# Reordering the opening of a fused attention and FFN kernel: casts, transposes, masks, table load and warm-up matmuls

## The chip, the cores and the metric

The kernel runs on one core of a Trainium2 chip. The core has TensorE (matmul, PE in the profile; its weight loads are PEld), VectorE (DVE), ScalarE (ACT), GpSimd (POOL) and SyncE (SP), which here only issues DMAs. The engines work through their own instruction queues in order and wait for one another by semaphores. The metric is the device time of one execution in microseconds (us), taken as the median over runs. Lower is better.

## The reference

A causal linear attention with decay is computed in blocks of 64 positions, with a running state per batch and head, and its output goes through a SwiGLU feed-forward layer:

```python
# q, k, v: (4 batches, 8 heads, 768 positions, 64); lam: one decay per head
for b in range(nb):                      # blocks of 64 positions
    intra = einsum('bhic,bhjc->bhij', qb, kb) * Dmask     # lam ** (i - j), causal
    intra = einsum('bhij,bhjd->bhid', intra, vb)
    inter = einsum('bhid,bhde->bhie', qb * lam_pow, kv_state)
    out[:, :, sl] = intra + inter
    kv_state = lam_block * kv_state + einsum('bhsd,bhse->bhde', kb * rev_pow, vb)
x = out.transpose(0, 2, 1, 3).reshape(3072, 512)
g = x @ w_gate                           # 512 x 1536
y = (silu(g) * (x @ w_val)) @ w_out      # 1536 x 512
```

Inputs and output are float32. The kernel multiplies in bfloat16 and accumulates in float32.

## The kernel before

The attention is done in 12 groups. A group is 256 positions of one batch with all 8 heads, held as two blocks of 128. The FFN is done in six steps of two groups each (512 tokens), with d_ff cut into 12 pieces of 128 columns (`fc`). For each piece TensorE makes the gate product (`ffn_gate`, L519) and the value product (`ffn_val`, L534) with four matmuls each; ScalarE applies silu (L523) and VectorE multiplies (L537). `ffn_out` (L552) multiplies by w_out.

The schedule is written out by hand: instructions go to each engine's queue in the order of the Python code, and the tile framework only adds semaphores. PSUM has eight banks, taken in a ring, and `ring[0] = n` sets where the ring goes on.

The opening is the part up to the list `steps`. It does groups 0 and 1 and the first two FFN pieces, while the loads are still coming in:

- **Loads.** SP issues lam, then k, q and v of groups 0 and 1 in halves of four heads, then weight pieces (`w_piece`). The two q halves of group 0 are issued from ScalarE's queue. Each half is 256 KB.
- **Warm-up.** TensorE starts with matmuls on constants: 30 tiny ones (L166, 8 columns), then `warm_up` ones of 512 columns (L131), with the small product that spreads lam over the partitions between them (L168). Later `warm_into` puts further constant matmuls of 256 columns (L172) between the real work.
- **Decay tables.** ScalarE takes the logarithm of lam (L180, L182) and then makes four tables `qdec` (L188), the factors `dec` for v (L614) and `lamgrp` for the state (L615) with exponentials. These need one activation table set; silu needs another, which is loaded by `preload_act_table_set("silu_and_others")` (L639).
- **Casts.** `cast_half(g, c, fns)` (L278) casts half `c` of k with `fns[0]` and of q with `fns[1]` to bfloat16; `None` leaves one out. `ACTC`, `DVEC` and `POOLC` are the copies of ScalarE, VectorE and GpSimd.
- **Transposes.** `pe_transpose(g, c, order, warm)` transposes on TensorE (L294). For k (`i == 0`) ScalarE copies the result out of PSUM (L296); for q (`i == 1`) VectorE does and multiplies by `qdec` (L300). `order` says which of the two comes first.
- **Scores and masks.** `scores` (L331) makes the products of q and k and leaves the causal masks (L338, VectorE) in a list; `run_later(n)` issues the next n of them.
- **v and state.** `v_scale` (L243, GpSimd) scales v by `dec`. `upd_mm` (L387) makes the state update of a group from k and the scaled v, and `upd_copy` copies it out on ScalarE: part 0 is `kvn` (L401), part 1 the two `ups` copies (L409). `state` (L426 to L437) goes on with them on GpSimd.
- **Output.** `intra` (L479) multiplies the masked scores by v, `inter` (L466) adds the part of the state. `guard` (L450) is a one-column copy on ScalarE that orders one after the other. `evac` (L491) copies the result into `xt`, the FFN's input.

## Time and profile before

| what | value |
|---|---|
| median of 5 runs | 228.05 us (227.53, 227.58, 228.05, 228.51, 229.45) |
| the profiled execution | 228.05 us |
| its span, first to last instruction | 226.3 us |
| TensorE busy in the span | 218.5 us |
| ScalarE, VectorE, GpSimd busy | 106.4, 90.8, 89.4 us |
| read from HBM, written | 28.31 MB, 6.29 MB |
| DMA share of 16 engines, in each microsecond from 3 to 15 | 1.04 to 1.15 |

The profile shows one execution. Times in it count from the start of the span. A row of the timeline gives start, duration, engine, source line, operation, the tile that is written and the one that is read, and in brackets how long the engine was idle before and what ended that. The durations of matmuls are modelled at their ends and overlap when matmuls are pipelined, so the distance of their starts says more than their sum.

### The profile page before, as it was taken

To read this page: it belongs to the slowest core of one execution; us is meant where nothing else is said; L and a number is where in the kernel's file an instruction comes from. 1 tells how busy PE (TensorE), PEld (TensorE's weight loads), DVE (VectorE), ACT (ScalarE), POOL (GpSimd) and SP (SyncE) were. 2 spreads that over 40 slices of the span, in tenths; PEclk is the share of its full clock that TensorE was granted. 3 is DMA by queue.
4 is the path that set the end of the run, shared out by engine and by line. 5 is a ranking of instruction groups with operands and counts; after the bars stand their busy time and mean duration, and the time that the engine had idled before them with its cause. 6 is when DMAs were issued, how large, how long until landed. Compare 5 with 4: busy or idle time off the path is not lost.

```text
span 226.3 us, 6040 instructions
## 1 busy us (share of the span) xinstructions
PE 218.5 (97%) x2504; PEld 122.6 (54%) x2504; DVE 90.8 (40%) x158; ACT 106.4 (47%) x211; POOL 89.4 (40%) x132
## 2 busy tenths in 40 slices
PE   8789999998999999999999999999999999999994
PEld 4566456886886555554544544544544444444442
DVE  2664358566753711733335262253242123222200
ACT  5878584854563353555454453453433423322321
POOL 6684737709593130979563092192150000000000
PEclk9999999999999999999999999999999999999999
DMA  6999999999997979396788838907101101101122
GB/s 196 345 330 363 369 353 322 241 156 303 402 262 161 245 209 269 77 226 167 180 194 217 217 83 219 247 3 139 49 1 46 49 0 46 46 3 46 46 93 93
DMA packets 88028, 39.70 MB, mean 175 GB/s; under 512 B 57666, under 2 KB 83522, under 8 KB 88002
## 3 DMA queue, kind: packets, MB, share of 16 engines
q1 hardware_dynamic: 83490, 32.58, 55.9%
q10 hardware_dynamic: 4512, 6.75, 8.2%
q8 instruction: 19, 0.31, 0.6%
q14 instruction: 7, 0.06, 0.1%
HBM read 28.31 MB, written 6.29 MB: 153 GB/s over the span
## 4 chain that ended last, share of the span: by engine, by line
PE 83%; DMA 8%; SPq 3%; POOL 3%; issue 1%; ACT 0%; DVE 0%; DVEq 0%; POOLq 0%
PE bank L552 28%; PE bank L519 25%; PE bank L534 24%; DMA v<-in_v_dram 8%; SPq L100 3%; POOL v_s L243 2%; PE bank L479 2%; PE bank L466 2%; PE bank L387 1%; PE bank L357 1%; PE bank L331 0%; PE bank L294 0%; POOL kvf L426 0%; POOL kvs L429 0%; ACT qkt L296 0%
## 5 line engine op out<-in xcount | busy, mean ns | idle before, releaser
L537 DVE TENSOR_TENSOR h<-sil,bank 128x512 bf16<-128x512 bf16 (+1 forms) x91 | 51.6, 575 | 103.9 <-PE bank L534 83.1
L519 PE MATMUL bank<-xt,wg_sb 128*128 128x512 bf16 (+1 forms) x364 | 77.2, 335 | 0.0
L534 PE MATMUL bank<-xt,wv_sb 128*128 128x512 bf16 (+1 forms) x364 | 77.1, 335 | 0.0
L523 ACT ACTIVATE sil<-bank 128x512 bf16<-128x512 f32 (+1 forms) x91 | 46.3, 514 | 42.6 <-PE bank L519 38.2
L552 PE MATMUL bank<-wo_sb,h 128*128 128x512 bf16 (+2 forms) x300 | 65.5, 371 | 0.0
L534 PEld LDWEIGHTS <-wv_sb 128*128 128x128 bf16 x364 | 35.5, 98 | 26.8
L519 PEld LDWEIGHTS <-wg_sb 128*128 128x128 bf16 x364 | 34.4, 98 | 26.0 <-DVE xt L491 0.2
L552 PEld LDWEIGHTS <-h 128*128 128x128 bf16 x300 | 28.7, 98 | 32.7
L554 ACT COPY osb<-bank 128x512 f32<-128x512 f32 (+1 forms) x24 | 14.0, 582 | 56.5 <-PE bank L552 56.5
L243 POOL TENSOR_TENSOR v_s<-v,dec 128x1024 bf16<-128x1024 f32 (+1 forms) x15 | 24.2, 1616 | 31.5 <-DMA v<-in_v_dram 31.3
L426 POOL TENSOR_TENSOR kvf<-kvs,ups 128x256 f32<-128x256 f32 x8 | 6.8, 849 | 29.5 <-ACT ups L409 26.8
L338 DVE TENSOR_TENSOR ssb<-bank,causal 128x512 bf16<-128x512 f32 x24 | 15.5, 684 | 4.6 <-PE bank L331 4.6
L491 ACT CAST xt<-bank 128x512 bf16<-128x512 f32 x19 | 11.6, 657 | 4.0 <-PE bank L479 3.1
L435 POOL CAST kvn<-kvf 64x256 bf16<-64x256 f32 x24 | 11.6, 482 | 1.5
L426 POOL TENSOR_TENSOR kvf<-kvf,ups 128x256 f32<-128x256 f32 x16 | 11.6, 724 | 0.6
L409 ACT COPY ups<-bank 128x256 f32<-128x256 f32 (+1 forms) x24 | 9.5, 450 | 1.4 <-PE bank L387 1.0
L263 ACT CAST qk<-kraw 128x1024 bf16<-128x1024 f32 x9 | 9.4, 1045 | 0.6 <-DMA qraw<-in_q_dram 0.5
L362 DVE TENSOR_TENSOR ssb<-bank,causaln 128x512 bf16<-128x512 f32 x12 | 8.2, 688 | 1.4 <-PE bank L357 1.3
L265 DVE TENSOR_TENSOR qk<-qraw,qdn 128x1024 bf16<-128x1024 f32 x6 | 7.6, 1267 | 2.0 <-DMA qraw<-in_q_dram 2.0
L387 PE MATMUL bank<-v_s,qk 64*64 64x64 bf16 x352 | 5.7, 195 | 1.8 <-POOL v_s L243 1.8
L479 PE MATMUL bank<-ssb,v_s 64*64 64x128 bf16 (+1 forms) x384 | 7.1, 207 | 0.3 <-ACT guard L450 0.3
L479 PEld LDWEIGHTS <-v_s 64*64 64x64 bf16 x384 | 5.7, 105 | 1.4 <-issue 0.7
(67 smaller groups left out, 121.5 us busy)
## 6 DMA issues: line engine op xcount, KB each, us to landing
out_dram<-osb ACTq DMA_DIRECT2D x23, 256.0 KB, 2.8
v<-in_v_dram SPq DMA_DIRECT2D x18, 256.0 KB, 4.5
woraw<-in_moe_w_out_dram SPq DMA_DIRECT2D x6, 512.0 KB, 8.1
kraw<-in_k_dram SPq DMA_DIRECT2D x24, 128.0 KB, 3.6
qraw<-in_q_dram SPq DMA_DIRECT2D x24, 128.0 KB, 3.4
wraw<-in_moe_w_gate_dram SPq DMA_DIRECT2D x5, 512.0 KB, 7.1
wraw<-in_moe_w_val_dram SPq DMA_DIRECT2D x5, 512.0 KB, 7.1
kraw<-in_k_dram SPq DMA_DIRECT2D x4, 512.0 KB, 6.4
```

What stands on the lines that cost most here:

```text
L243: eng.tensor_tensor(out=st[("vs", g)][:, h0:h1], in0=st[("v", g)][:, h0:h1].rearrange("p h (s d) -> p h s d", s=2), in1=vfac(g, h0, h1), o ...
L338: nc.vector.tensor_tensor(out=ssb[:, h2, 2 * c:2 * c + 2].rearrange("p a s n -> p a (s n)"), in0=sp[(c, h2)].rearrange("p (a x) -> p a x", ...
L426: nc.gpsimd.tensor_tensor(out=o, in0=f, in1=u, op=ALU.add)
L435: nc.gpsimd.tensor_copy(out=o[64 - h2 * 64:128 - h2 * 64], in_=f[h2 * 64:h2 * 64 + 64])
L479: nc.tensor.matmul(op[r][h2 * 64:h2 * 64 + 64, cols(g, hp, s)], v_s[ps, 2 * hp + h2, s], ssb[ps, h2, hp * 2 + s] if g >= NAT0 else ssb[ps, ...
L491: fns[r](out=xt[:, g % 2, :, r].rearrange("p h (m s) -> p h s m", s=2) if g < NAT0 else xt[:, g % 2, :, :, r * M:r * M + M], in_=op[r].rea ...
L519: nc.tensor.matmul(gp[:, 0:N], wg_sb[:, mc, fs], xt[:, b0 // 2:b1 // 2, mc].rearrange("p g b n -> p g (b n)"), start=(mc == 0), stop=(mc = ...
L523: nc.scalar.activation(sil[:, 0:N], gp[:, 0:N], AF.Silu)
L534: nc.tensor.matmul(vp[:, 0:N], wv_sb[:, mc, fs], xt[:, b0 // 2:b1 // 2, mc].rearrange("p g b n -> p g (b n)"), start=(mc == 0), stop=(mc = ...
L537: nc.vector.tensor_tensor(out=h_sb[:, fc % FH, b0:b1].rearrange("p b n -> p (b n)"), in0=sil[:, 0:N], in1=vp[:, 0:N], op=ALU.mult)
L552: nc.tensor.matmul(ps, st[("h", t, fc // FH)][:, fc % FH, b], wo_sb[:, fc, c0:c1], start=(fc == 0), stop=(fc == FC - 1))
L554: fn(out=osb[:, c0:c1], in_=ps)
```

## The change

All of it lies in the opening. No load, no shape and no arithmetic is changed.

- The lead-in has 40 tiny matmuls instead of 30, one 512-column warm-up ahead of the lam product instead of two, and three behind it instead of four.
- Group 0, first half: ScalarE casts k ahead of the first two `qdec` tables, not behind them. k is transposed ahead of q. The transposes stand ahead of the exponential of `dec`, and `lamgrp` moves behind the transposes of the second half.
- Group 0, second half: k is cast on GpSimd instead of ScalarE, and the two casts stand behind the first transposes.
- Of the constant matmuls of 256 columns between the real work, five go and three come in, two of those ahead of group 1's first transposes and one ahead of its last scores.
- The copy of group 0's state update (`upd_copy(0, (1,))`) moves up, to directly behind the first guard.
- Group 1, second half: the transposes of k and of q are taken apart; the load of the silu table set and `inter(0)` stand between them. The load stood ahead of `intra(0)`.
- The first gate weights are cast on VectorE instead of GpSimd.

```diff
--- before.py
+++ after.py
@@ -161,12 +161,12 @@
 
     lam_ps = bank()
     b = bank()
-    for n in range(30):
+    for n in range(40):
         r = slice(n % 2 * 64, n % 2 * 64 + 64)
         nc.tensor.matmul(b[r, 0:8], warm[r, 0:64], warm[r, 0:8], start=True, stop=True, skip_group_check=True)
-    warm_up(2)
+    warm_up(1)
     nc.tensor.matmul(lam_ps[:, 0:H], ones[:, 0:128], lam_row, start=True, stop=True)
-    warm_up(4)
+    warm_up(3)
     def warm_into(b, n, cols=256):
         for _ in range(n):
             nc.tensor.matmul(b[:, 0:cols], warm[:, 0:128], warm[:, 0:cols], start=True, stop=True)
@@ -607,55 +607,53 @@
     w_piece(1, 2)
     w_piece(2, 4)
     w_piece(4, 6)
-    cast_half(0, 0, (None, DVEC))
+    cast_half(0, 0, (ACTC, DVEC))
     qdec_table(0)
     qdec_table(1)
-    cast_half(0, 0, (ACTC, None))
+    ring[0] = 0
+    pe_transpose(0, 0, (0, 1), warm=1)
     nc.scalar.activation(dec, dec, AF.Exp)
-    nc.scalar.activation(lamgrp, lnp, AF.Exp, scale=float(2 * BLK))
-    cast_half(0, 1, (None, DVEC))
-    ring[0] = 0
-    pe_transpose(0, 0, warm=1)
-    cast_half(0, 1, (ACTC, None))
+    cast_half(0, 1, (POOLC, DVEC))
     qdec_table(2)
     qdec_table(3)
-    scores(0, (0,), 3)
+    scores(0, (0,), 2)
     run_later(1)
     v_scale(0, nc.gpsimd, 0, H // 2)
     v_scale(0, nc.gpsimd, H // 2, H)
     pe_transpose(0, 1)
+    nc.scalar.activation(lamgrp, lnp, AF.Exp, scale=float(2 * BLK))
     run_later(1)
     scores(0, (1,), 3)
     cast_half(1, 0, (ACTC, POOLC))
     run_later(1)
     ring[0] = 4
+    warm_into(banks[4], 2)
     pe_transpose(1, 0, (0,))
     ring[0] = 0
     up = [bank() for _ in range(2)]
-    warm_into(up[0], 1)
     upd_mm(0, up)
     run_later(1)
     upd_copy(0, (0,))
-    nc.scalar.preload_act_table_set("silu_and_others")
     ring[0] = 2
     st[("op", 0)] = [bank() for _ in range(2)]
     warm_into(st[("op", 0)][0], 1)
     ring[0] = 5
     pe_transpose(1, 0, (1,))
     cast_half(1, 1, (POOLC, POOLC))
-    warm_into(st[("op", 0)][0], 1)
     intra(0, True)
     guard(0)
+    upd_copy(0, (1,))
     ring[0] = 4
     scores(1, (0,))
     run_later(1)
     ring[0] = 6
-    pe_transpose(1, 1, (0, 1), warm=1)
+    pe_transpose(1, 1, (0,))
+    nc.scalar.preload_act_table_set("silu_and_others")
+    inter(0, False)
+    pe_transpose(1, 1, (1,))
     run_later(1)
-    inter(0, False)
-    upd_copy(0, (1,))
     ring[0] = 6
-    scores(1, (1,))
+    scores(1, (1,), 1)
     evac(0, (ACTC, ACTC))
     v_scale(1, nc.gpsimd, 0, H // 2)
     v_scale(1, nc.gpsimd, H // 2, H)
@@ -666,11 +664,11 @@
     upd_mm(1, up)
     upd_copy(1, (0,))
     (wg0, wg0r), (wv0, wv0r) = w_raw.pop(0), w_raw.pop(0)
-    POOLC(out=wg0, in_=wg0r)
+    DVEC(out=wg0, in_=wg0r)
     POOLC(out=wv0, in_=wv0r)
     ring[0] = 4
     st[("op", 1)] = [bank() for _ in range(2)]
-    warm_into(st[("op", 1)][0], 2)
+    warm_into(st[("op", 1)][0], 1)
     intra(1, True)
     guard(1)
     ring[0] = 2
```

## Prediction

> **What bounds the kernel now.** I read the busy shares first, then TensorE's own waits, then the chain of waits in the first 30 us, then the timeline of the opening. The page:

> ```profile
> PE 218.5 (97%) x2504; PEld 122.6 (54%) x2504; DVE 90.8 (40%) x158; ACT 106.4 (47%) x211; POOL 89.4 (40%) x132
> ...
> PE   8789999998999999999999999999999999999994
> ```

> TensorE is busy in 97% of the 226.3 us span; only the first slices are thinner. From about 15 us on it runs back to back, so the time is "when does TensorE enter its steady stream" plus a constant. Of TensorE's waits this is the longest entry:

> ```profile
> PE bank L387 <- POOL v_s L243: 1.8, 2, 1.1
> ```

> Two waits for a scaled v: 0.7 us at 13.76 (group 1) and 1.06 us at 51.3 (group 4). The second depends on a load queued behind ScalarE's cast for group 3 at 40.81, which follows TensorE's own progress, so it moves with the opening. The first decides. The chain of waits (start, duration, what):

> ```profile
> 7.79 5.52 DMA v<-in_v_dram
> 13.31 0.07 issue
> 13.37 1.06 POOL v_s L243
> 14.43 0.04 issue
> 14.47 0.38 PE bank L387 x24
> 14.86 0.33 PE bank L172 x2
> 15.18 0.57 PE bank L479 x32
> 15.75 0.54 PE bank L519 x4
> ```

> The reader should see what is *not* in it: no cast, transpose, mask or table load of group 0. The chain runs through SP's loads, the landing of group 1's second v half at 13.31, its scaling on POOL, and only then TensorE. The loads run without a gap (DMA share 1.04 to 1.15 in every microsecond from 3 to 15, about 340 GB/s). Timeline rows for the steps below (start, duration, engine):

> ```profile
> 3.23 1.89 PE L131 MATMUL bank<-const-bfloat16-1.0 128*128 128x512 bf16 x4
> ...
> 4.65 0.60 ACT L278 CAST qk<-kraw 128x512 bf16<-128x512 f32 x1
> ...
> 6.94 2.05 POOL L243 TENSOR_TENSOR v_s<-v,dec 128x512 bf16<-128x512 f32 x2 [2.61 <-DMA v<-in_v_dram]
> ...
> 10.62 1.28 ACT L639 ACT_TABLE_LOAD   x1
> ...
> 11.92 0.16 ACT L450 COPY guard<-bank 128x1 f32<-128x1 f32 x1
> ...
> 13.07 1.36 ACT L491 CAST xt<-bank 128x512 bf16<-128x512 f32 x2
> ...
> 14.37 0.61 POOL L669 CAST wg_sb<-wraw 128x512 bf16<-128x512 f32 x1
> ...
> 19.79 0.43 DVE L689 CAST wv_sb<-wraw 128x512 bf16<-128x512 f32 x1 [2.08 <-DMA wraw<-in_moe_w_val_dram]
> ```

> **The change part by part.** No DMA issue is added, removed or moved on SP or ScalarE's queue, so v of group 1 should still land at 13.31; that caps everything.

> *Lead-in.* Ten more tiny matmuls at 0.027 us each (30 in 0.8 us) add 0.27; one 512-column warm-up fewer takes off 0.40 (starts 1.74 and 2.14). The lam product moves from 2.70 to about 2.57 and ScalarE's logarithm from 3.33 to 3.20, after the table load's end at 3.11. Gain there 0.13 us, hidden.

> *First casts.* ScalarE's k cast now stands ahead of the two decay tables. Its data land at 4.55, so ScalarE idles from 3.60, casts 4.58 to 5.18, builds the tables to 6.0 (each 0.41 apart) and copies k's transposes at about 5.95, against 6.07 now. K is transposed first, at 5.25 instead of 5.55; q's transposes slip from 4.91 to about 5.85. VectorE's multiply for q starts near 6.31 instead of 5.65 and ends 6.80, so the first scores start near 6.86 instead of 6.71: +0.15. TensorE idles between about 4.34 and 5.25, where it had no gap. The exponentials of dec end near 6.7, in time for v at 6.78, so POOL's v_scale keeps its 6.94.

> *Second half of group 0.* The k cast goes to POOL: 0.61 us at 6.08, inside POOL's 2.61 us of idle before v lands; with that cover gone it would push v_scale. VectorE's q cast slips from 5.23 to about 6.75 and the transposes from 7.05 to about 7.25; two ScalarE items less in front of their copy (cast 0.52, one small exponential 0.16) give that back: copy at 7.92 against 7.88. Second scores near 8.65 against 8.55: +0.1.

> *Warm fillers.* The 256-column fillers cost 0.11 to 0.16 each. Two go into the idle gap before 9.30; two ahead of group 0's update and output disappear, so its intra product starts near 10.4 instead of 10.66. All of this is ahead of the wait for v.

> *Table load.* It leaves 10.62, where it held up the guard to 11.92, and goes behind the k copy of group 1. Guard near 11.27, the two state copies (0.66) to 12.03, k copy to 12.6, load 12.5 to 13.8, then the two output copies 13.8 to 15.16, where they ended at 14.43. Their reader is the gate matmul at 15.69, or about 15.55 after the change: 0.4 us of slack where there was 1.26. Queued behind them on ScalarE are kvn of group 1 (0.37, to 15.44) and the second guard, which cannot start before TensorE's intra(1) ends near 15.6. So the load lands in slack, barely. [...] By the trace a load costs 1.28: the guard starts 0.01 after it ends. [...] I take the row.

> *Group 1.* Masks end as now, near 14.75: k copy ends 12.6 in both. wg0's cast moves to VectorE: 0.43 (the L689 row of that shape), at 14.7, ahead of an evacuation that waits for TensorE until 15.8 anyway. POOL's wv0 cast rises from 14.92 to its landing at 14.7. Both hidden; without that cover the gate matmul would wait. One filler less at L172 lies *behind* the wait for v: the chain prices two at 0.33, so −0.16.

> *What is late next.* Weights: the L689 cast ends at 20.22 and its matmul starts at 20.50. TensorE can be early by 0.28 us at most before it waits there, so the 0.16 passes, and no opening could give over 0.3.

> Sum against the profiled execution (228.05: span 226.3 and 1.75 around it; the median of the five is the same 228.05): −0.16, **227.9 us**.

> **The clock, which no row prices directly.** The four 512-column matmuls at 3.23 start 0.43 us apart; in the steady stream they run at 0.22. So the first 5 us run at half rate, although the granted-clock column says 1.00 there: it does not show this stretch. The 256-column filler at 5.33 takes 0.42, the one at 9.54 0.27, so the change of rate falls near 5.7. [...] Before, TensorE is busy without a gap from 0.84 to 6.3[...]. After, two of six dense warm-ups are gone and there is a 0.9 us hole at 4.34; the gapless stretch is 3.5 us[...]. Bounds: [...] a gain is excluded, as what comes earlier is hidden behind v. At the other end, half rate until the steady stream: TensorE's 6.1 us of busy time between 6.2 and 14.5 grows by about half, 3 us, against 2.2 of idle there, so about 1 us late[...]. [...] I take 0, nearest to the row in which TensorE at 66% and 42% busy (6 to 7, 8 to 9 us) kept its rate.

> **The rivals.**
> 1. *The likeliest: hidden, −0.16.* 227.9, within 227.3 to 228.6. For it: the chain. Chance 0.58.
> 2. *Slower: the clock rises later.* Place: the hole before the first transpose. It decides once half rate lasts beyond about 12 us: +1.2 there,[...] 229.2 to 230.7. [...] against: the fillers that remain. Chance 0.20.
> 3. *ScalarE becomes the bound behind the later load.* Slip beyond the 0.4 us of slack[...], 228.3 to 228.9. Against: the guard row. Chance 0.14; a third of it counted as slower with the spread of runs.
> 4. *Faster by more:* the wait of 1.06 us before 52.35 also goes, because v of group 4 gets issued earlier against TensorE: 227.9 − 1.06 = 226.8. Against: its queue position hangs on ScalarE's cast at 40.81, which shifts along. Chance 0.08.

> **How the numbers follow.** The bound of 0.5% is 1.14 us, about what a measurement of this kernel can tell from no change (the five runs lie 1.9 us apart). Faster: rival 4 with what falls short, 0.07. Slower: rival 2 and a third of rival 3, 0.25. Same: 0.68. The range runs from 227.0 (it leaves out rival 4's centre) to 229.9 (it takes in rival 3 and half of rival 2). The likeliest case alone is 227.3 to 228.6.

> **What would show it.** Right: v of group 1 lands at 13.2 to 13.4, POOL's scaling still releases TensorE near 14.47, one filler follows it, the gate matmul starts near 15.55, and the second load's end is followed by the output copies within 0.05. Wrong: 512- or 256-column matmuls at half spacing after 9 us (rival 2); the gate matmul released by ScalarE's xt copy (rival 3); no wait before group 4's update (rival 4). A landing of v that moves by over 0.3 us would break the first step of the argument.

## The result and the profile after

The changed kernel takes 230.05 us at the median of 27 runs (228.55 to 232.69), the kernel before 228.02 us (48 runs). The ratio is 1.0084, 95% interval 1.0067 to 1.0101: slower by 0.8%, where 227.9 us and "no change" were forecast. Ratios and medians are separate estimates (the ratios leave out executions far above a kernel's fastest), so where a ratio is not the quotient of two medians, its interval counts.

The profiled execution took 230.18 us with a span of 228.5. The page and TensorE's waits (total us, times, longest) after the change:

```profile
PE 220.7 (97%) x2510; PEld 123.7 (54%) x2510; DVE 92.9 (41%) x159; ACT 105.9 (46%) x210; POOL 89.0 (39%) x132
```

```profile
PE bank L294 <- ACT qk L278: 0.9, 1, 0.9
...
PE bank L534 <- issue: 0.6, 1, 0.6
...
PE bank L479 <- DVE ssb L338: 0.5, 1, 0.5
PE bank L294 <- DVE qk L278: 0.5, 1, 0.5
```

TensorE is as busy as before, 97%, and its busy time has grown by 2.2 us although it does less filler work. And the entry that decided before, the wait for POOL's scaled v, is gone from the list. What stands there instead are waits for casts of group 0. The chain of waits of the first 30 us (start, duration, what) agrees:

```profile
1.22 3.48 DMA kraw<-in_k_dram
...
5.24 0.90 ACT qdec L188 x2
...
6.17 0.59 ACT qkt L296
6.76 0.47 DVE qkt L300 x2
7.23 1.10 DVE qk L278
...
8.38 1.03 PE bank L294 x8
9.42 0.64 PE bank L172 x3
...
10.09 0.64 PE bank L331 x14
...
17.44 0.54 PE bank L519 x4
```

In the profile before, the loads carried the opening to 13.3 us and group 0 was hidden behind them. Now the chain leaves the loads at 4.7 us, with the first k, and runs on through group 0's casts, tables, copies and transposes to the first gate matmul. The timeline shows why these steps are long (start, duration, engine):

```profile
3.07 1.46 PE L131 MATMUL bank<-const-bfloat16-1.0 128*128 128x512 bf16 x3
5.39 0.61 PE L294 MATMUL bank<-ident,qk 128*128 128x128 bf16 x4 [0.86 <-ACT qk L278]
...
9.21 0.85 PE L172 MATMUL bank<-const-bfloat16-1.0 128*128 128x256 bf16 x3
...
12.01 0.28 PE L172 MATMUL bank<-const-bfloat16-1.0 128*128 128x256 bf16 x1
...
17.38 0.61 PE L519 MATMUL bank<-xt,wg_sb 128*128 128x256 bf16 x4
```

```profile
7.15 1.18 DVE L278 CAST qk<-qraw 128x512 bf16<-128x512 f32 x1
```

```profile
7.00 2.23 POOL L243 TENSOR_TENSOR v_s<-v,dec 128x512 bf16<-128x512 f32 x2 [0.23 <-ACT dec L615]
...
11.43 2.06 POOL L243 TENSOR_TENSOR v_s<-v,dec 128x512 bf16<-128x512 f32 x2 [0.19 <-DMA v<-in_v_dram]
```

```profile
14.55 1.28 ACT L651 ACT_TABLE_LOAD   x1
15.85 1.35 ACT L491 CAST xt<-bank 128x512 bf16<-128x512 f32 x2
```

Three things are to be seen. The three fillers at 9.21 take 0.85 us, 0.21 apart: half rate. The single one at 12.01 takes 0.28 where one at half rate takes 0.42: full rate. The trace's clock record puts the change of rate at 11.64 us in this execution, and at 5.73 in the one before. Second, TensorE stands idle for 0.86 us ahead of the first transposes. Third, VectorE's cast takes 1.18 us for the work that takes 0.43 elsewhere, and it lies beside GpSimd's scaling of v, whose two halves also take 2.23 instead of 2.05.

Where the time went, by the same matmul in both profiles: the first gate matmul starts at 17.38 instead of 15.69, 1.69 later. The update of group 4 starts only 0.77 later, because the wait of 1.06 in front of it is gone. A wait of 0.49 for a mask stands behind it, and from there on the delay is 1.45. Near 70 us TensorE idles for 0.61 with no releaser (the entry "issue" above), and the delay becomes 2.2; at the last matmul it is 2.1.

### The profile page after: what moved, and what is told of

Same layout as the page of the kernel before. It is cut to its first block, busy times and chain, and to the rows that moved or that the text cites. A ratio compares the mean times of both kernels' runs of the same rounds, so it can differ in the third digit from the quotient of the medians.

```text
span 228.5 us, 6051 instructions
## 1 busy us (share of the span) xinstructions
PE 220.7 (97%) x2510; PEld 123.7 (54%) x2510; DVE 92.9 (41%) x159; ACT 105.9 (46%) x210; POOL 89.0 (39%) x132
## 3 DMA queue, kind: packets, MB, share of 16 engines
q10 hardware_dynamic: 4512, 6.75, 8.0%
## 4 chain that ended last, share of the span: by engine, by line
PE 93%; DVE 2%; DMA 2%; ACT 1%; issue 1%; SPq 0%; DVEq 0%
PE bank L519 28%; PE bank L534 27%; PE bank L552 27%; PE bank L479 2%; PE bank L466 2%; PE bank L331 2%; DMA kraw<-in_k_dram 2%; PE bank L294 1%; PE bank L387 1%; PE bank L357 1%; PE bank L172 1%; DVE qkt L300 1%; DVE qk L278 0%; ACT qkt L296 0%; ACT qdec L188 0%
## 5 line engine op out<-in xcount | busy, mean ns | idle before, releaser
L519 PE MATMUL bank<-xt,wg_sb 128*128 128x512 bf16 (+1 forms) x364 | 77.2, 335 | 0.0
L519 PEld LDWEIGHTS <-wg_sb 128*128 128x128 bf16 x364 | 34.4, 98 | 25.9
L243 POOL TENSOR_TENSOR v_s<-v,dec 128x1024 bf16<-128x1024 f32 (+1 forms) x15 | 23.5, 1578 | 31.7 <-DMA v<-in_v_dram 31.3
L338 DVE TENSOR_TENSOR ssb<-bank,causal 128x512 bf16<-128x512 f32 x24 | 15.6, 684 | 4.1 <-PE bank L331 4.1
L491 ACT CAST xt<-bank 128x512 bf16<-128x512 f32 x19 | 11.6, 655 | 3.8 <-PE bank L479 2.8
L435 POOL CAST kvn<-kvf 64x256 bf16<-64x256 f32 x24 | 11.6, 482 | 1.5
L426 POOL TENSOR_TENSOR kvf<-kvf,ups 128x256 f32<-128x256 f32 x16 | 11.6, 724 | 0.6
L265 DVE TENSOR_TENSOR qk<-qraw,qdn 128x1024 bf16<-128x1024 f32 x6 | 8.1, 1353 | 2.3 <-DMA qraw<-in_q_dram 2.3
L479 PE MATMUL bank<-ssb,v_s 64*64 64x128 bf16 (+1 forms) x384 | 7.5, 208 | 0.8 <-DVE ssb L338 0.5
L479 PEld LDWEIGHTS <-v_s 64*64 64x64 bf16 x384 | 5.8, 105 | 2.0 <-issue 1.2
L294 PE MATMUL bank<-ident,qk 128*128 128x128 bf16 x48 | 5.1, 257 | 1.3 <-ACT qk L278 0.9
```

Of the source, the lines that this page charges most:

```text
L243: eng.tensor_tensor(out=st[("vs", g)][:, h0:h1], in0=st[("v", g)][:, h0:h1].rearrange("p h (s d) -> p h s d", s=2), in1=vfac(g, h0, h1), o ...
L338: nc.vector.tensor_tensor(out=ssb[:, h2, 2 * c:2 * c + 2].rearrange("p a s n -> p a (s n)"), in0=sp[(c, h2)].rearrange("p (a x) -> p a x", ...
L426: nc.gpsimd.tensor_tensor(out=o, in0=f, in1=u, op=ALU.add)
L435: nc.gpsimd.tensor_copy(out=o[64 - h2 * 64:128 - h2 * 64], in_=f[h2 * 64:h2 * 64 + 64])
L479: nc.tensor.matmul(op[r][h2 * 64:h2 * 64 + 64, cols(g, hp, s)], v_s[ps, 2 * hp + h2, s], ssb[ps, h2, hp * 2 + s] if g >= NAT0 else ssb[ps, ...
L491: fns[r](out=xt[:, g % 2, :, r].rearrange("p h (m s) -> p h s m", s=2) if g < NAT0 else xt[:, g % 2, :, :, r * M:r * M + M], in_=op[r].rea ...
```

## The experiments

All ratios are to the kernel before, run beside each version (its median was 227.8 to 228.0). Times "back" are differences of medians to the changed kernel's 230.05; what the ratios make of them stands under "How the two causes meet". E1 to E4 undo or transplant one part. The first theory was the clock: fewer dense warm-ups and the hole in front of the transposes keep TensorE at half rate. Its rival was the order of the work, with the long cast.

**E1, the old lead-in in the changed kernel.**

```diff
-    for n in range(40):
+    for n in range(30):
-    warm_up(1)
+    warm_up(2)
     # lam product
-    warm_up(3)
+    warm_up(4)
```

> The changed kernel with the lead-in of before: 30 tiny matmuls, two 512-column warm-ups ahead of the lam product, four behind it. Clock theory (the lost dense warm-ups and the hole ahead of the first transposes keep TensorE at half rate until 11.6 us): the rate changes near 6 us again, the first gate matmul comes back from 17.4 to about 16.1, and the time is about 228.7, at most 0.4% over before. Order theory (k ahead of q, and VectorE's q cast of 1.18 us beside GpSimd's v_scale, make the opening late): the hole is shorter but the chain is not, 229.6 to 230.

Measured: 228.93 us, 1.0043 (1.0015 to 1.0070). The rate changed at 6.56 us (0.42 us for a filler ahead of it, three in 0.49 behind it), and 1.1 us of the 2.0 came back. The rest was still there, in the other wait:

```profile
5.72 0.42 PE L172 MATMUL bank<-const-bfloat16-1.0 128*128 128x256 bf16 x1
...
8.76 0.49 PE L172 MATMUL bank<-const-bfloat16-1.0 128*128 128x256 bf16 x3
```

```profile
PE bank L294 <- DVE qk L278: 0.7, 1, 0.7
```

So the clock is a cause, but not the only one.

**E2, the new lead-in alone in the kernel before** (the reverse of the diff above).

> The kernel before with the lead-in alone of the change: 40 tiny matmuls, one 512-column warm-up ahead of the lam product, three behind it. Clock theory by count of dense warm-ups: [...] +0.5 to +1.5 us, 228.5 to 229.5. Clock theory by the hole: no hole opens, as q is transposed at 4.9 without waiting for k, so 228.0 to 228.3. Order theory: 228.0, no change.

Measured: 228.38 us, 1.0023 (1.0002 to 1.0044). The rate changed at 9.46 us in the profile. The new lead-in alone costs about half a microsecond at the median. Here too a hole opens, since TensorE waits 0.7 us for the cast of k. The profile does not tell how much of the loss is the clock's: TensorE also stops for 0.82 us with no releaser, and the one wait for a scaled v that is left is that of group 4:

```profile
14.78 0.25 PE L331 MATMUL bank<-qkt 64*64 64x128 bf16 x3 [0.82 <-issue]
...
53.21 0.45 PE L387 MATMUL bank<-v_s,qk 64*64 64x64 bf16 x32 [0.79 <-POOL v_s L243]
```

**E3, VectorE's second q cast back to its early place in the changed kernel.**

```diff
     qdec_table(1)
+    cast_half(0, 1, (None, DVEC))
     ring[0] = 0
     pe_transpose(0, 0, (0, 1), warm=1)
     ...
-    cast_half(0, 1, (POOLC, DVEC))
+    cast_half(0, 1, (POOLC, None))
```

> The changed kernel with VectorE's q cast of group 0's second half put back ahead of the first transposes, so that it runs at about 5.3 us while GpSimd is idle. Clock theory: the half rate stays until about 11.6, and at most 0.3 us comes back, 229.8. Order theory: the cast takes 0.43 and not 1.18, the second transposes start near 7.5 instead of 8.4, and 0.7 to 0.9 us come back, 229.2.

Measured: 228.76 us, 1.0055 (1.0034 to 1.0076): 1.3 us back at the median. The cast is short again:

```profile
5.29 0.43 DVE L278 CAST qk<-qraw 128x512 bf16<-128x512 f32 x1 [1.04 <-DMA qraw<-in_q_dram]
```

and the second transposes start at 7.79 instead of 8.38. In this profile the rate changed between the fillers at 6.36 (0.21 apart) and those at 8.55 (0.11 apart), so its first gate matmul, at 16.34, owes a part to the clock.

**E4, the table load back to its old place in the changed kernel** (the `preload_act_table_set` line directly behind `upd_copy(0, (0,))`).

> The changed kernel with the load of the silu table set where it was, ahead of intra of group 0. Theory of the later load as a bound: ScalarE's two output copies no longer stand behind it, the gate matmul comes up to 0.5 us earlier, 229.5. Clock and order theories: the gate matmul is not released by ScalarE in the changed kernel (it follows TensorE's own intra product), so 230.0, no change, or slower by 0.3 where the guard waits for the load.

Measured: 230.03 us (6 runs), 1.0090 (1.0060 to 1.0120). No change is seen, within about 0.8 us by the intervals. The load in its later place is not what slows the kernel.

**E5, both parts back, E1 and E3 together.** This was to tell whether the two causes add up or are one.

> The changed kernel with both of the parts put back that gave time back alone: the lead-in of before (30, two, four) and VectorE's second q cast ahead of the first transposes. If clock and cast are the two causes and add up: 230.0 less 1.1 and 1.3, 227.7, no slower than before. If k ahead of q costs as well, or the two gains are one (both only let TensorE reach its wait for v): 228.3 to 228.7.

Measured: 228.01 us, 0.9996 (0.9976 to 1.0017). The whole loss is gone, with k ahead of q, the k cast on GpSimd, the later table load and the fewer fillers all still in. TensorE's list again has a wait for a scaled v, but not the one that ruled before. It lies ahead of group 4's update; in group 1 the scaling runs through both halves, and TensorE does not wait for it:

```profile
11.73 2.05 POOL L243 TENSOR_TENSOR v_s<-v,dec 128x512 bf16<-128x512 f32 x2 [0.16 <-DMA v<-in_v_dram]
...
52.07 0.45 PE L387 MATMUL bank<-v_s,qk 64*64 64x64 bf16 x32 [0.52 <-POOL v_s L243]
```

**E6, k ahead of q alone in the kernel before.**

```diff
-    cast_half(0, 0, (None, DVEC))
+    cast_half(0, 0, (ACTC, DVEC))
     qdec_table(0)
     qdec_table(1)
-    cast_half(0, 0, (ACTC, None))
     ...
-    pe_transpose(0, 0, warm=1)
+    pe_transpose(0, 0, (0, 1), warm=1)
```

> The kernel before with one thing of the change: in group 0's first half ScalarE casts k ahead of the two tables and k is transposed ahead of q. Lead-in, second half and all else as before. Order theory: the first scores start 0.3 to 0.5 later, and TensorE's wait for v of 0.7 us swallows it, 227.9; with the clock theory the hole ahead of the first transposes (from 5.1 to 5.35, short) matters little, 227.9 to 228.3. If k ahead of q is a cause by itself, 228.5 or more.

Measured: 227.93 us, 1.0001 (0.9982 to 1.0020). No cause by itself. But no wait for v swallows it in this profile: the scaling of group 1 ends at 13.43, and the first gate matmul starts at 15.18, earlier than before.

**E7, the later half alone:** the kernel before up to `scores(0, (1,), 3)`, the changed one from there on.

> The kernel before up to group 0's second scores, the changed kernel from there on: fillers, earlier state copies, later table load, parted transposes of group 1, gate weights cast on VectorE. The sum of the prediction for these parts: one filler fewer behind the wait for v, -0.16, 227.7. Theory of ScalarE as the bound behind the later load: +0.2 to +0.5, 228.2.

Measured: 227.75 us, 1.0008 (0.9983 to 1.0032). The forecast gain of 0.16 us lies inside the interval and is not shown. The profile caught one of two executions of 14 that took 229.8 us, and showed something unexpected. Windows (start:end, busy us of PE, PEld, DVE, ACT, POOL, then granted clock, DMA share, GB/s):

```profile
12.15:15.56 3.41, 2.31 (x82) 1.45 (x82) 2.69 (x6) 3.06 (x5) 1.93 (x3) 1.00 1.13 344
15.56:18.98 3.42, 3.42 (x40) 2.12 (x29) 1.15 (x2) 1.27 (x3) 1.23 (x2) 0.50 1.05 325
```

The clock had risen at 5.32, and fell back to half from 15.56 to 18.98, just when the first FFN products run. Against the same matmuls in the profile of before, the delay rises across it from 0.17 us to 1.57.

**E8, twelve more TensorE instructions in the kernel before** (six tiny matmuls ahead of `pe_transpose(1, 0, (0,))`), for the idle time near 70 us.

> The kernel before with six tiny matmuls more in an idle stretch of TensorE near 9.1 us, so that TensorE's queue holds 12 more instructions from there on, as many as in the changed kernel. Theory of the instruction fetch ([...] 0.6 us in the changed kernel's profile): +0.3 to +0.6, 228.3, and an idle time without a releaser near 69 us in the profile. Otherwise 227.9, no change.

Measured: 228.25 us at the median, 1.0004 (0.9983 to 1.0025), and no idle time without a releaser near 70 us in this one profile. The count of instructions alone did not bring it about there.

**E9, the new lead-in and k ahead of q together in the kernel before.**

> The kernel before with two parts of the change together: the new lead-in (40, one, three) and k ahead of q in group 0's first half. Alone the first cost 0.2% and the second nothing. Theory of the hole (fewer warm-ups end at 4.3, k's data come at 4.7, TensorE idles for 0.9 us[...]): more than the sum, 228.7 to 229.1. Theory that the two parts simply add: 228.3.

Measured: 228.85 us, 1.0035 (1.0019 to 1.0051). At the medians this is more than the sum of E2 and E6; the intervals alone would not tell it from the sum. The profile has the hole and the late clock (11.66 us) of the changed kernel:

```profile
PE bank L294 <- ACT qk L278: 0.9, 1, 0.9
```

**E10, the late q cast on ScalarE in the changed kernel** (`cast_half(0, 1, (POOLC, ACTC))`): same place, but not beside GpSimd's work on VectorE.

> The changed kernel with the q cast of group 0's second half in its late place, but on ScalarE instead of VectorE (behind the exponential of dec, 0.6 us), so that nothing of VectorE's copies runs beside GpSimd's v_scale. Contention theory (the cast took 1.18 us instead of 0.43 because v_scale ran): the transposes start near 7.6 instead of 8.4, 228.9 to 229.3. Place theory (any cast behind the first multiply is too late): 229.8 to 230.2.

Measured: 229.03 us, 1.0049 (1.0028 to 1.0071), so 1.0 us of E3's 1.3 comes back with the cast still behind the first multiply:

```profile
6.58 0.61 ACT L278 CAST qk<-qraw 128x512 bf16<-128x512 f32 x1
```

The second transposes start at 7.63, and GpSimd's scaling takes 2.06 again. (The rate changed at 9.04 us in this profile, so its later times owe a part to the clock.) It is mainly the neighbour, not the place, that made the cast expensive.

**E11, only the hole filled in the changed kernel** (`warm_up(5)` behind the lam product instead of `warm_up(3)`).

> The changed kernel with five instead of three 512-column warm-ups behind the lam product, so that TensorE is busy up to 5.2 us; the 40 tiny ones and the single warm-up ahead of it stay. Clock theory by the hole: as with the old lead-in, rate changes at 6 to 8 us, 228.9. Theory that the dense matmuls of the first two microseconds matter: still late, 229.5 to 230.

Measured: 229.53 us at the median, 228.0 to 232.2, ratio 1.0057 (1.0034 to 1.0080). In the profile the rate changed at 5.29 us, so filling the hole does bring the clock forward. With it came something else: the transposes at full rate let the late cast start at 6.47, ahead of the scaling of v (6.97), and it took 0.59:

```profile
6.47 0.59 DVE L278 CAST qk<-qraw 128x512 bf16<-128x512 f32 x1
```

But the clock fell back, as in E7:

```profile
12.12:15.53 3.41, 2.29 (x73) 1.34 (x71) 2.23 (x5) 3.12 (x5) 1.86 (x3) 1.00 1.11 336
15.53:18.95 3.42, 3.22 (x32) 2.04 (x32) 1.22 (x3) 1.27 (x3) 1.45 (x3) 0.50 0.97 317
```

A fall of 3.42 us at half rate in a span of 228.0 us gives a mean clock of about 0.992 (an estimate from this profile: 1 less half of 3.42 by 228.0; the execution's clock is 0.991). Seven of its 22 executions have 0.990 to 0.993, and they take 229.7 to 232.2 us; the other 15 have a median of 229.0, as E1.

**E13, the hole filled and the lost fillers put back in the changed kernel.** E11 left open where the fall comes from; three more runs were made for it.

> The changed kernel with the hole filled (five 512-column warm-ups behind the lam product) and with the five 256-column fillers put back that it had lost. Theory of the window[...]: no fall at 15.5, fewer executions over 230, median 228.9 to 229.1 as with the old lead-in. If the fall comes from something else (q cast, the wait for v): spread and median as with the hole filled alone, 229.5.

Measured: 228.91 us, 1.0042 (1.0019 to 1.0065), the median of E1. One execution of 15 has a lowered clock, and it is the profiled one, at 232.88 us: there the fall came elsewhere, at 71.62 us, after this (the last bracket is the idle time before the row):

```profile
67.99 0.38 PE L534 MATMUL bank<-xt,wv_sb 128*128 128x256 bf16 x2
70.79 0.39 PE L534 MATMUL bank<-xt,wv_sb 128*128 128x256 bf16 x2 [2.42 <-issue]
```

TensorE stopped for 2.42 us inside a group of four matmuls, with nothing in the profile to wait for. The trace's DMA records hold one packet of the kind "instruction", 16 KB, that starts at 65.35 us and took 3.95 us; the ones before and after it took 1.03 and 1.19. TensorE went on 1.49 us after its end. The same stop, shorter, is in the changed kernel (0.61), in E3 (1.44) and in E14 (0.98), behind such packets that took 1.1 to 1.2 us (1.18 in the changed kernel), and E5, E7 and E10 have some of 2.6 to 3.2 us and no stop behind them. So the length of a packet alone does not decide. That these packets have to do with the stops is an estimate from these times; no run showed it.

**E12, E14 and E15, versions that might beat both.** E12 is the kernel before with its tiny matmuls replaced by two more `warm_up` ones. E14 is E6 with `warm_into(up[0], 5)` instead of 1 ahead of group 1's state update. E15 joins the lead-in of E12 with these fillers.

> The kernel before with its 30 tiny matmuls replaced by two more 512-column warm-ups (0.85 us for 0.80), four ahead of the lam product and four behind. Clock theory: [...] 227.5, and fewer executions over 229. Rival: in this kernel the clock is early enough for the wait for v to hide it, 227.9, no change. Could be slower by 0.1 where the lam product comes later.

> The kernel before with k ahead of q in group 0's first half and four more 256-column fillers ahead of group 1's state update (0.43 us, in front of the wait for v of 0.7 us). Theory of the window: no execution falls back to half rate, the median goes to 227.6 to 227.8. Rival: the fillers delay the update in executions in which v lands early, 228.0 to 228.2.

> The kernel before with its tiny matmuls replaced by two 512-column warm-ups and four more 256-column fillers ahead of group 1's state update. Theory of the window: the rate changes near 5 us and does not fall back, so the executions over 229 of the dense lead-in alone go, median 227.5. Rival as for the other: 228.0.

Measured: 227.90 us (0.9998, 0.9976 to 1.0020), 227.81 us (1.0007, 0.9987 to 1.0026) and 227.84 us (1.0001, 0.9987 to 1.0015). None beats the kernel before at the median. E12's profile has the change of rate at 5.02 us and a span of 225.7, yet 4 of its 14 executions fell back (clock 0.990 to 0.991) and took 229.1 to 229.3. With the four fillers none did: 0 of 14 and 0 of 22, against 4 of 44 of the kernel before in the same session. E15's executions lie between 227.5 and 228.5, those of before between 227.0 and 229.6. That is a narrower spread, on few executions, and not a faster kernel.

## Why the prediction was wrong, point by point

- **The step that failed under both causes: "v of group 1 should still land at 13.31; that caps everything".** The slack that was to hide the slips was read from one execution. In the profile before, TensorE does wait for v:

```profile
14.47 0.38 PE L387 MATMUL bank<-v_s,qk 64*64 64x64 bf16 x24 [0.71 <-POOL v_s L243]
```

  Of the other 16 profiles only E7's has this wait (0.78 us). E6, E8, E12, E14 and E15, which are close to the kernel before, have none, and their first gate matmul starts at 15.2 to 15.5 us, ahead of the 15.69 of before, with medians of 227.8 to 228.3 us. So the cover of 0.7 us is there in some executions only; how many is not known. Even the whole of it would not have been enough: TensorE came to the update of group 1 at 15.94 instead of 13.76.
- **The step that failed first: "VectorE's q cast slips from 5.23 to about 6.75 and the transposes from 7.05 to about 7.25".** The cast came 0.40 later than that (7.15), but the duration was the term that was mis-sized most: 0.43 was carried over from a row in which GpSimd was idle, and it took 1.18. The transposes started at 8.38. This is worth 1.3 us at the medians (E3). The prediction put the k cast on GpSimd "inside POOL's 2.61 us of idle" and asked only whether v_scale would be pushed; it did not ask which VectorE work had been moved onto v_scale. The changed kernel's cast, from 7.15 to 8.33, lies across both halves of the scaling:

```profile
7.00 1.05 POOL L243 TENSOR_TENSOR v_s<-v,dec 128x512 bf16<-128x512 f32 x1 [0.23 <-ACT dec L615]
...
8.00 1.23 POOL L243 TENSOR_TENSOR v_s<-v,dec 128x512 bf16<-128x512 f32 x1
```

  The first half of the scaling takes its usual 1.05 us, the cast beside it ends at 8.33, 0.28 after that half, and the second half takes 1.23. The cast is long again in E1, E4 and E13 (1.17, 1.31 and 1.29 us), and each time it ends 0.28 to 0.29 us after the first half, wherever it started. With GpSimd idle beside it, it takes 0.43 in E3 and E5. By what means the two engines slow each other is not shown. The trace of before held a hint, too: one 128x512 cast of GpSimd ran beside VectorE's of the same weights (0.43, at 19.79) and took 0.87, where its others take 0.61:

```profile
19.82 0.87 POOL L689 CAST wv_sb<-wraw 128x512 bf16<-128x512 f32 x1 [2.91 <-DMA wraw<-in_moe_w_val_dram]
```

```profile
4.81:8.22 3.41, 2.31 (x27) 1.65 (x27) 1.48 (x3) 2.87 (x7) 1.83 (x3) 1.00 1.15 346
8.22:11.63 3.41, 3.21 (x33) 2.18 (x33) 2.65 (x7) 1.20 (x3) 2.99 (x5) 1.00 1.15 346
```

  The stretch at 2.31 us busy was not followed by the change, the one at 3.21 was. In all 15 profiles that hold a record of the clock, TensorE was busy for 3.0 to 3.4 us in the stretch just before the change; earlier ones were at 2.8 us or less, or held a part of the tiny matmuls (3.13 in the changed kernel, from 1.40 to 4.81). That the busy time of such a stretch decides is an estimate from these figures; no run tested it apart from the rest. The rival's deciding point, "beyond about 12 us: +1.2", assumed that up to there the wait for v would swallow the rest. There was no wait left. The upper ends of rivals 2 and 3, 230.7 and 228.9 us, were the author's estimates; no row showed them.
- **How the two causes meet.** Put back alone they give 1.1 us (E1) and 1.3 (E3) at the medians, together 2.0 (E5), which is the whole loss. By the ratios it is 0.9, 0.7 and 2.0 us, each uncertain by 0.6 to 0.7 (an estimate from the intervals), so whether they simply add is not shown. They also touch: the multiply for q in front of the late cast (6.75 in the changed kernel) waits for transposes at half rate, and E11, at full rate there, has the cast at 6.47, before the scaling starts at 6.97.
- **The later table load:** costed at nothing, and E4 agrees. The row was right: the load at 14.55 takes 1.28 and the output copies start 0.02 after its end.
- **First casts, lead-in gain, group 1:** the k cast waited for its data (1.14 us of idle, 0.98 forecast), the first scores started at 7.29 instead of the forecast 6.86, because the q transposes ran at half rate (four in 0.63 at 6.01; E11, at full rate there, has the scores at 6.60). The single filler behind the wait, the forecast's only gain, cannot be seen: E7 is at 1.0008.
- **The landing of v** was expected at 13.2 to 13.4, or the first step breaks. GpSimd's scaling of group 1 starts at 11.43 and runs through both halves without a wait, so v landed by about 12.5. The step broke: the load was earlier, and TensorE was not there to use it.
- **Rival 4,** the wait before group 4 that would vanish, did vanish, and a mask's wait of 0.49 came in its place. The prediction had this wait move along with the opening. It did not: ScalarE's cast for group 3 came 1.70 us later (42.51), but the scaling of v for group 4 only 0.77 later (51.15 instead of 50.38). That took back a part of the loss and made no gain, since TensorE itself arrived 1.7 us later.

Not settled: which part of the lead-in (tiny ones, one warm-up ahead, one behind) matters most beyond the hole, and what stops TensorE near 70 us. The stop there makes 0.8 of the 2.1 us in the profile of the changed kernel; how often it comes in executions without a profile is not known. The loss does not need it: E4 has the same TensorE instructions, no such stop in its profile, and takes 229.96 us there.

## What to carry to other kernels

Before a cast is moved, look at what the other engines do at the time it lands on: here the same VectorE cast took 0.43 us with GpSimd idle and 1.18 beside GpSimd's scaling of v. Work that is hidden behind a wait is free only up to the length of the wait, and two slips share that length. Warm-up matmuls are a part of the schedule: count the gap that a new order opens in front of the first real matmul (here 0.86 us, with half rate up to 11.64), and compare executions one by one, since the clock changed anywhere from 4.8 to 13.9 us in these profiles. A wait that is to hide something should stand in more than one profile.

## What was not expected of the hardware

- **The clock fell back behind a stretch in which TensorE was far from idle.** In E7 and E11 TensorE was busy for 2.31 and 2.29 of 3.41 us (68% and 67%, by modelled durations) just before the fall, and then ran at half rate for 3.42 us. The busy share does not decide it: E1 was busy for 2.03 us from 6.55 to 9.97, and did not fall. The cause of the falls stays open.

```profile
6.55:9.97 3.42, 2.03 (x47) 1.30 (x45) 3.23 (x7) 2.08 (x7) 3.11 (x5) 1.00 1.15 346
```

- **The change to full rate spread from 4.8 to 13.9 us** over the profiles. Kernels with the old, the dense or a filled lead-in had it between 4.8 and about 8; those with the new one between 6.6 and 13.9, so the two overlap a little.
- **The granted-clock column of the profile shows 1.00 for the first half-rate stretch** (from 8.22 to 11.63 in the changed kernel, where fillers stand 0.21 us apart), and 0.50 only for a later fall (15.56 to 18.98 in E7). The distance of equal matmuls is the safer reading.
- **TensorE stood idle with nothing in the profile to wait for.** Behind the first 5 us the 17 profiles have 14 such stops of 0.2 us or more: ten near 14 us (0.22 to 0.82) and four near 70 (0.61, 0.98, 1.44 and 2.42). All 14 end 1.2 to 1.6 us after the end of a 16 KB packet of the DMA kind "instruction" (in the changed kernel at 69.35, and TensorE goes on at 70.59). That TensorE waits for such packets there is an estimate from these times; it was not shown.
